# Reordering the first batch of an attention, Fourier mix and feed-forward kernel by changing the durations in its order model

## The chip, the cores and the metric

The kernel runs on one core of one Trainium2 chip. A core has five engines that work side by side, each through its own queue in program order: TensorE (PE, with its weight loads shown apart as PEld), VectorE (DVE), ScalarE (ACT), GpSimd (POOL) and SyncE (SP). POOL and SP also issue the DMAs. The metric is the device time of one execution in microseconds.

## The reference

Eight batches of 12 heads, 448 positions and 64 features per head. A squared-ReLU attention is followed by a Fourier mix over both axes, a normalization and a feed-forward layer, with the un-normalized sum added back:

```python
scores = q @ k.T / sqrt(64)
x = (maximum(scores, 0) ** 2 / 448) @ v        # heads side by side: (8, 448, 768)
u = x + real(fft(fft(x, axis=1), axis=2))
un = (u - mean(u)) / sqrt(var(u) + 1e-6)
out = u + maximum(un @ w_ch1, 0) @ w_ch2        # 768 -> 3072 -> 768
```

## The kernel before

Everything is on the chip at once as a pipeline over batches. For batch b, `load_group` fetches queries, keys and values of four heads at a time (three groups per batch) by DMAs that POOL issues. The heads are turned so that features lie on partitions: for batches 0 and 1 on TensorE (`turn_on_pe`, line 505, copied back at line 510), from batch 2 on by a VectorE reordering copy (line 469) and a transposing DMA on SP (line 481). `attention` makes, for each pair of heads m (six per batch) and each quarter c of the keys, a score (line 736, two matmuls on half the array each). ScalarE takes the ReLU (line 761), VectorE or ScalarE the square (lines 776, 773), and four quarters are multiplied with the values (line 718). `fold` scales the product and adds and subtracts its mirrored halves, which halves the work of the Fourier mix.

The mix multiplies with cosine and sine tables: `build_dft` makes them at the start, from indices that POOL writes (`dft_indices`, lines 245 to 251), with VectorE (lines 304 to 306) and ScalarE sines (line 310). For half of the channels the negated table is needed (line 333). Batch 0's channel products (`first_channels`, line 1187) run while its attention is going on. Then `first_tail` does the row products (lines 823, 827), the statistics (847), the scale, the normalization (900 to 905), the turn on TensorE (926) and the unload (941) for four tiles of rows. Its end makes the first feed-forward group ready. Feed-forward groups (`ffn`, lines 1452, 1477, 1503, 1583) are groups of 384, 512, 384 and then 256 rows. Their matmuls are what TensorE does most of the time, and attention of later batches is put between them.

The order of all instructions is not written by hand. Each piece is a Python generator that asks `need(engine, duration, dependencies, buffers)`. `Streams.run` picks, again and again, the request that could start first by its own clock of each engine, and the pieces issue their instructions in that order. So the durations (`mm`, `act`, `dve`, `SWITCH`, `LATENCY`), the times added to a load before it counts as ready (`ready`), and the ranks given to `sch.add` decide only the order in each engine's queue. On the chip every instruction still waits for its real data. A gate with the constant `LEAD` keeps later batches' attention from running too far ahead of the feed-forward work.

While TensorE has nothing to do in the order model before the first channel products are complete, `warming` issues short matmuls on zeros (line 1661), so that its clock stays up. There are three score banks (`BS`, one of them taken by the first channel products) and two feed-forward banks (`BF`), which the transposes, the value products and the fourth row tile also use. The software DMA queue of POOL works in order and has eight semaphores in turn, so a ninth DMA waits for the first.

The line that gives the time at which loads count as ready, and the keys' transposing DMA that waits in the model for the queries' landing:

```python
ready[i][x].t = sch.dma(e, GRP, 360e3, "sw") + (1.5 if g else 0.0, 3.0, 14.0, 7.0)[min(b, 3)]
...
for x in range(2):
    e = yield need("SP", 0.8, [e + LATENCY["DVE"]], [BQT] if x == 0 else [])
    nc.sync.dma_start_transpose(out=t, in_=qk[x])
    e = sch.dma(e + 0.5, R * 2048, 180e3)
```

Of the kernel before, what the change touches and what calls it, by code (L numbers as in the profile page):

```python
# [11 lines left out]
AF = mybir.ActivationFunctionType  # L12
# [46 lines left out]

LATENCY = {"PE": 0.28, "ACT": 0.18, "DVE": 0.16, "POOL": 0.2, "SP": 0.1}  # L60


class Streams:
# [29 lines left out]
    def run(self):  # L93
        end = {}
        while self.streams:
# [36 lines left out]
            self.engine[eng] = start + dur  # L132
# [28 lines left out]
SWITCH = 0.13  # L161
# [3 lines left out]
def kernel(  # L165
# [132 lines left out]
    def build_dft():  # L298
# [27 lines left out]
        for m in range(3):  # L326
# [5 lines left out]
            e = yield need("DVE", 0.3, [dft_ready])  # L332
            nc.vector.tensor_scalar(chan_neg[:, m], chan[m][:, :, KH:], -1.0, None, op0=ALU.mult)
            dft_ready.t = chan_ready[m].t = e + LATENCY["DVE"]

# [26 lines left out]
    def load_group(i, which=(0, 1, 2)):  # L362
# [3 lines left out]
        for x, (nm, src) in enumerate((("q", q), ("k", k), ("v", v))):  # L366
# [54 lines left out]
    def loading():  # L421
# [11 lines left out]
        yield from load_group(NG + 2, (2,))  # L433
        yield from load_w2([1, 2, 3])
# [22 lines left out]
    def turning():  # L457

        for b in range(B):
            for g in range(NG):  # L460
# [62 lines left out]
    def fold(b, m, F, av, give, av_end):  # L523
# [4 lines left out]
        def leave():  # L528
# [10 lines left out]
            if b == 0:  # L539
# [119 lines left out]
    def attention(b, left=None):  # L659
# [9 lines left out]
        while pa < NB:  # L669
# [38 lines left out]
            for part in ("scores", "values") if few else ("values", "scores"):  # L708
# [19 lines left out]
                for i in range(p, p + n):  # L728
                    m, c = divmod(i, 4)
                    qT, kT, flat = turned[b][m // 2]  # L730
                    wide = R if b < 2 else 128
                    k0 = (2 * c + m % 2) * R
                    sc = BS.take()
                    for h in range(2):
                        ps = slice(h * Dh, (h + 1) * Dh)
                        nc.tensor.matmul(sc[:wide, h, 0:S].rearrange("k (c q) -> k c q", c=4),  # L736
                                         lhsT=flat[ps, k0:k0 + wide], rhs=qT[ps, m % 2],
                                         start=True, stop=True)
# [4 lines left out]
                    if b == 0 and i == NB - 1:  # L743
                        first_scores.t = e
# [8 lines left out]

    def squares(b, scs, sqs):
        for i, sc, t in scs:
            e = yield need("ACT", act(2 * S) - 0.03, [t + LATENCY["PE"]], [BSQ])
# [42 lines left out]
    def first_tail(pcs):  # L799
# [88 lines left out]
        def norm(t, hf, en):  # L888
# [5 lines left out]
            d = {"ACT": act(D // 2), "DVE": dve(D // 2), "POOL": 2.0}[en]  # L894
# [12 lines left out]
            t_un[t][hf] = e + LATENCY[en]  # L907
            if min(t_un[t]) or en == "POOL":
                half_un[ch][i].t = max(t_un[t])
# [25 lines left out]
        def unload(t, en):  # L935
            n, idn, c0, w = turned_cols(t)
            g = groups[0][2]
            src = pts[t][0][:, :, 0:384].rearrange("p h (m w) -> p h m w", w=128)[:, :, :, 0:w]
            dst = g[:, :, c0:c0 + w].rearrange("p (h m) w -> p h m w", h=2)
            last = yield need(en, (act if en == "ACT" else dve)(6 * w), [done[t][0]])  # L940
            (nc.scalar.copy if en == "ACT" else nc.vector.tensor_copy)(dst, src)
            BS.give(pts[t][0], last)
# [774 lines left out]
```

## Time and profile before

| what | value |
|---|---|
| median of 3 runs | 584.73 us (584.64 to 585.35) |
| the profiled execution | 584.67 us, span 582.8 us |
| mean granted clock of TensorE | 0.997 |
| TensorE busy | 572.9 us (98% of the span) |
| VectorE, ScalarE, POOL busy | 406.4, 335.0, 133.7 us |
| moved by DMA | 81.85 MB, mean 140 GB/s |

The page has six parts: busy time of each engine, the span in 40 slices, the DMA queues, the chain of work that ended last, the costliest groups of instructions, and the DMA issues. Besides there are views that answer a question: busy time in chosen windows, a timeline of one engine, who waited for whom, and groups by line. In a timeline a row gives the start and length in microseconds, the engine, the line, the operation, output and inputs, and in brackets the idle time before it and what ended that. Rows of the same kind in a row are merged (x5). Matmuls overlap in the pipeline, so the length of one is more than its share of TensorE's time.

### The profile page before, as it was taken

The numbers are of one execution on the slowest core, as the hardware profiler recorded it, in microseconds if no ns is written. First come the engines' busy times: TensorE is split into PE (matmuls) and PEld (weight loads), VectorE is DVE, ScalarE is ACT, GpSimd is POOL, SyncE is SP. The second block draws the span as 40 slices with busy tenths as digits, with TensorE's granted clock in tenths as the row PEclk, the third lists the DMA queues.
The fourth block names the chain that finished last, engine by engine and source line by source line (L and its number), as shares of the span: only waits on it lengthen the run. The fifth ranks groups of instructions, "written<-read, shape, count | busy, mean of one in ns | idle before, by whom it ended". The sixth has DMA issues, their size and how long they took to land.

```text
span 582.8 us, 11457 instructions
## 1 busy us (share of the span) xinstructions
PE 572.9 (98%) x4476; PEld 365.7 (63%) x4476; DVE 406.4 (70%) x927; ACT 335.0 (57%) x511; POOL 133.7 (23%) x188
## 2 busy tenths in 40 slices
PE   8999999999999999999999999999999999999997
PEld 7566556544455546556857667568577786868684
DVE  5978667986669988787787878987946852222222
ACT  5866873587745787676668748777654340304040
POOL 8534021411115313421333032303300230000000
PEclk9998999999999999999999999999999999999999
DMA  9999999776947997699579987993433353031201
GB/s 120 206 211 227 222 210 134 173 131 95 181 57 189 207 172 168 116 216 167 122 123 207 180 153 147 200 176 115 126 75 100 118 151 99 30 94 36 79 30 55
DMA packets 133493, 81.85 MB, mean 140 GB/s; under 512 B 77504, under 2 KB 128704, under 8 KB 133440
## 3 DMA queue, kind: packets, MB, share of 16 engines
q0 software_dynamic: 40320, 33.63, 38.2%
q1 hardware_dynamic: 93120, 47.50, 36.3%
q8 instruction: 35, 0.57, 0.4%
q14 instruction: 18, 0.15, 0.1%
HBM read 62.91 MB, written 26.25 MB: 153 GB/s over the span
## 4 chain that ended last, share of the span: by engine, by line
PE 88%; DVE 6%; ACT 4%; issue 1%; POOL 0%; DVEq 0%; ACTq 0%; POOLq 0%
PE psF L1452 37%; PE psF L1583 26%; PE psS L736 6%; PE psF L718 5%; PE psF L1503 3%; PE psF L1477 3%; PE psS L1212 2%; ACT sq L761 2%; DVE sq L776 2%; PE psS L718 1%; PE psS L823 1%; PE psS L1026 1%; PE psS L1187 1%; PE psF L505 0%; ACT un L1087 0%
## 5 line engine op out<-in xcount | busy, mean ns | idle before, releaser
L1452 PE MATMUL psF<-unT,w 128*128 128x256 bf16 (+2 forms) x1728 | 229.8, 291 | 1.2 <-ACT unT L999 0.9
L1452 PEld LDWEIGHTS <-w 128*128 128x128 bf16 x1728 | 165.9, 98 | 61.6 <-issue 11.5
L761 ACT ACTIVATE sq<-psS 112x896 bf16<-112x896 f32 x192 | 164.4, 918 | 38.4 <-PE psS L736 38.0
L1426 ACT ACTIVATE hT<-psF 128x512 bf16<-128x512 f32 (+3 forms) x169 | 87.9, 532 | 116.6 <-PE psF L1452 115.8
L776 DVE TENSOR_TENSOR sq<-sq 112x896 bf16<-112x896 bf16 x161 | 100.6, 638 | 16.6 <-ACT sq L761 15.6
L1583 PEld LDWEIGHTS <-hT 128*128 128x128 bf16 x792 | 76.0, 98 | 54.4 <-issue 5.8
L1438 DVE TENSOR_TENSOR o<-psF,o 128x384 f32<-128x384 f32 x92 | 50.9, 553 | 44.8 <-PE psF L1583 39.6
L1583 PE MATMUL psF<-w,hT 128*128 128x384 bf16 x462 | 81.7, 326 | 0.3 <-DVE hT L1424 0.2
L736 PE MATMUL psS<-qkT 64*128 64x448 bf16 (+1 forms) x384 | 51.6, 359 | 1.2 <-ACT qkT L510 0.4
L718 PE MATMUL psF<-sq,vn 112*64 112x448 bf16 x320 | 37.9, 358 | 0.3 <-DVE o L1438 0.3
L557 DVE TENSOR_SCALAR xT<-psF 128x224 bf16<-128x224 f32 x58 | 19.8, 383 | 26.3 <-PE psF L718 26.2
L376 POOL DMA_DIRECT2D vn<-in_v_dram x24 | 17.3, 720 | 76.0 <-PE psS L736 67.7
L1059 POOL TENSOR_TENSOR u<-tp,xn 112x385 f32<-112x385 f32 (+2 forms) x14 | 13.3, 953 | 93.1 <-DVE tp L1041 81.5
L1583 PE MATMUL psF<-wsum,hT 128*128 128x384 bf16 x198 | 34.6, 326 | 0.0
L736 PEld LDWEIGHTS <-qkT 64*128 64x128 bf16 (+1 forms) x384 | 15.9, 102 | 28.7 <-issue 21.2
L376 POOL DMA_DIRECT2D qn<-in_q_dram x21 | 15.5, 739 | 69.9 <-DVE qkr L469 49.6
L718 PEld LDWEIGHTS <-vn 112*64 112x64 bf16 x384 | 17.8, 109 | 21.4 <-issue 13.7
L773 ACT ACTIVATE sq<-sq 112x896 bf16<-112x896 bf16 x31 | 29.5, 956 | 0.5
L1068 DVE BATCH_NORM_STATS2 stats<-u 112x6 f32<-112x384 f32 (+2 forms) x56 | 28.4, 541 | 0.0
L1087 ACT ACTIVATE un<-u,nmr,rstd 112x768 bf16<-112x768 f32 (+2 forms) x22 | 22.4, 1025 | 7.3 <-DVE nmr L1074 5.0
L1477 PE MATMUL psF<-w,hT 128*128 128x384 bf16 x144 | 25.1, 326 | 0.0
L1503 PE MATMUL psF<-w,hT 128*128 128x384 bf16 x144 | 24.7, 326 | 0.0
(166 smaller groups left out, 612.6 us busy)
## 6 DMA issues: line engine op xcount, KB each, us to landing
out_dram<-o SPq DMA_DIRECT2D x56, 192.0 KB, 2.2
vn<-in_v_dram POOLq DMA_DIRECT2D x24, 224.0 KB, 5.9
qn<-in_q_dram POOLq DMA_DIRECT2D x21, 224.0 KB, 5.3
kn<-in_k_dram POOLq DMA_DIRECT2D x21, 224.0 KB, 5.5
w<-in_moe_w_ch_dram POOLq DMA_DIRECT2D x12, 384.0 KB, 14.5
w<-in_moe_w_ch_dram POOLq DMA_DIRECT2D x4, 1152.0 KB, 20.5
utop<-u SPq DMA_DIRECT2D x12, 336.0 KB, 3.1
o<-utop SPq DMA_DIRECT2D x16, 192.0 KB, 3.8
```

What stands on the lines that cost most here:

```text
L376: nc.gpsimd.dma_start(out=t, in_=src[b, hs].rearrange("h (p j) d -> p h (j d)", j=4))
L718: nc.tensor.matmul(av[h * Dh:(h + 1) * Dh, 0:S], lhsT=vn[:, c, h0 + h, :], rhs=sq[:, h, :], start=(c == 0), stop=(c == 3))
L736: nc.tensor.matmul(sc[:wide, h, 0:S].rearrange("k (c q) -> k c q", c=4), lhsT=flat[ps, k0:k0 + wide], rhs=qT[ps, m % 2], start=True, stop= ...
L761: nc.scalar.activation(r, sc[:R, :, 0:S], AF.Relu)
L773: nc.scalar.activation(r, r, AF.Square)
L776: nc.vector.tensor_tensor(r, r, r, op=ALU.mult)
L1426: nc.scalar.activation(hs, ps, AF.Relu)
L1438: nc.vector.tensor_tensor(o, pc[:, 0:DH], o, op=ALU.add)
L1452: nc.tensor.matmul(ph[:, i * N:(i + 1) * N], lhsT=w1_sb[m][hf][:, (jj + i) * 128:(jj + i + 1) * 128], rhs=unT[:, m, 0:N], start=(m == 0), ...
L1477: nc.tensor.matmul(pc[:, 0:DH], lhsT=block(j, c), rhs=w2(j, hf), start=(j == 0), stop=(j == JC - 1))
L1503: nc.tensor.matmul(pc[:, 0:DH], lhsT=block(2 * i + k, c), rhs=weights[i], start=(start and i == 0), stop=(i == KP - 1), skip_group_check=True)
L1583: nc.tensor.matmul(pc[:, 0:DH], lhsT=lhs[i], rhs=rhs[i], start=(start and i == 0), stop=(i == KP - 1), skip_group_check=True)
```

## The change

Batch 0's attention becomes two streams: `first_attention` issues scores one at a time, `first_values` multiplies each quarter of the keys with the values as soon as that quarter is squared. Constants of the order model change: matmul, ScalarE and switching durations are shorter, `OVERLAP` lets an engine take the next instruction a little before the end of the last, the extra times of loads from batch 2 on go from 14 and 7 to 2 and 1, `LEAD` goes from 2.6 to 2.8. The negation of the tables moves from VectorE to POOL, the index writing goes ahead of the identity and of the first values' load, the last pair's scaling in batch 0 and the last unload are split over ScalarE and VectorE, the fourth tile's statistics go ahead of the third's scale, the fourth tile's copies behind its unload. Three of the four loads of the second weight matrix wait for the third tile's normalization. From batch 2 on the keys' transposing DMA counts as ready when the copies are done, not when the queries' transpose has landed. The second weight matrix counts as free for overwriting after the last whole chunk, not after each.

```diff
+OVERLAP = {"ACT": 0.12, "DVE": 0.07}
...
-            self.engine[eng] = start + dur
+            self.engine[eng] = start + max(dur - OVERLAP.get(eng, 0.0), 0.5 * dur)
...
-    return n / 2400 + 0.006
+    return n / 2400 + 0.002
...
-    return n / 1200 + 0.2
+    return n / 1200 + 0.17
...
-SWITCH = 0.13
+SWITCH = 0.1
...
-            e = yield need("DVE", 0.3, [dft_ready])
-            nc.vector.tensor_scalar(chan_neg[:, m], chan[m][:, :, KH:], -1.0, None, op0=ALU.mult)
-            dft_ready.t = chan_ready[m].t = e + LATENCY["DVE"]
+            sch.add(negative(m, dft_ready.t), (0, 0))
+
+    def negative(m, t):
+        e = yield need("POOL", 0.4, [t])
+        nc.gpsimd.tensor_scalar(chan_neg[:, m], chan[m][:, :, KH:], -1.0, None, op0=ALU.mult)
+        dft_ready.t = chan_ready[m].t = e + LATENCY["POOL"]
...
-            ready[i][x].t = sch.dma(e, GRP, 360e3, "sw") + (1.5 if g else 0.0, 3.0, 14.0, 7.0)[min(b, 3)]
+            ready[i][x].t = sch.dma(e, GRP, 360e3, "sw") + (1.5 if g else 0.0, 3.0, 2.0, 1.0)[min(b, 3)]
             if i == 0 and x == 1:
-                yield need("POOL", 0.7)
-                make_identity(nc, ident)
-            if i == 0 and x == 2:
                 e = yield need("POOL", 1.1)
                 dft_indices()
                 indices_ready.t = e + LATENCY["POOL"]
+                yield need("POOL", 0.7)
+                make_identity(nc, ident)
...
+        yield need("POOL", 0.0, [first_norms])
         yield from load_w2([1, 2, 3])
...
-                ts = []
+                ts, copied = [], e + LATENCY["DVE"]
                 for x in range(2):
-                    e = yield need("SP", 0.8, [e + LATENCY["DVE"]], [BQT] if x == 0 else [])
+                    e = yield need("SP", 0.8, [copied], [BQT] if x == 0 else [])
...
-            if b == 0:
+            if b == 0 and m == MC - 1:
+                t1 = yield need("ACT", act(HS), [av_end], [BX[m]])
+                nc.scalar.activation(xa[0], xa[1], AF.Copy, scale=1.0 / (64.0 * S))
+                t = yield need("DVE", dve(HS), [av_end])
+                nc.vector.tensor_scalar(xb[0], xb[1], 1.0 / (64.0 * S), None, op0=ALU.mult)
+                t = yield need("DVE", 2 * dve2(NS), [t1 + LATENCY["ACT"]])
+            elif b == 0:
...
+    def first_attention():
+        F, sqs = [], {}
+        for i in range(4 * MC):
+            m, c = divmod(i, 4)
+            e = yield need("PE", mm(S) + 2 * SWITCH, [turned_at[0][m // 2][m % 2]], [BS])
+            sc = score(0, i)
+            if i == 4 * MC - 1:
+                first_scores.t = e
+            sqs[i] = [None, Cell(), None]
+            sch.add(squares(0, [(i, sc, e - SWITCH)], sqs), (0.2, 0.2))
+            if c == 3:
+                if m % 2 == 1:
+                    BQT.free.append(e)
+                sch.add(first_values(m, F, sqs), (0.1, 0.1))
+
+    def first_values(m, F, sqs):
+        vn, h0 = loads[m // 2][2], 2 * m % HG
+        for c0, c1 in ((0,1),(1,2),(2,3),(3,4)):
+            e = yield need("PE", (c1 - c0) * mm(S) + 2 * SWITCH, [sqs[4 * m + c][1] for c in range(c0, c1)] + [ready[m // 2][2]],
+                           [BF] if c0 == 0 else [])
+            if c0 == 0:
+                av = BF.take()
+            for c in range(c0, c1):
...
+                for h in range(2):
+                    nc.tensor.matmul(av[h * Dh:(h + 1) * Dh, 0:S], lhsT=vn[:, c, h0 + h, :], rhs=sq[:, h, :],
+                                     start=(c == 0), stop=(c == 3))
...
         yield from stats(3, 0)
+        yield from stats(3, 1)
+        yield from aggregate(3)
         yield from scale(2)
         yield from norm(2, 0, "POOL")
-        yield from stats(3, 1)
-        yield from aggregate(3)
...
+        yield from turn(3, 0)
+        yield from unload(3, "ACT", 0)
+        yield from unload(3, "DVE", 1)
         yield from copy(3, 0, "ACT")
-        yield from turn(3, 0)
-        yield from unload(3, "DVE")
         yield from copy(3, 1, "DVE")
...
-            w2_free.t = e + LATENCY["PE"]
+            if c == WHOLES[b][-1]:
+                w2_free.t = e + LATENCY["PE"]
...
-    LEAD, MIXED, SPARE, ELASTIC = 2.6, 1, 0.5, (1, 99)
+    LEAD, MIXED, SPARE, ELASTIC = 2.8, 1, 0.5, (1, 99)
...
-        sch.add(attention(0), (0, 0))
+        sch.add(first_attention(), (0, 0))
```

More of the change, by code (lines that the diff above doesn't have):

```diff
@@ L729, in attention @@
                     m, c = divmod(i, 4)
[L730 to L738, printed above, removed]
+                    sc = score(b, i)
                     scs.append((i, sc, e - SWITCH - (4 * mm(S) + SWITCH if values and few else 0.0)
@@ L752, in attention, with score @@
                 yield from fold(bv, mv, Fv, av, give, av_end)
+    def first_attention():
[20 more added lines that the diff above has]
+            for c in range(c0, c1):
+                sq, _, at = sqs.pop(4 * m + c)
+                sq_ids.append((e, at))
+                BSQ.free.append(e)
+                for h in range(2):
+                    nc.tensor.matmul(av[h * Dh:(h + 1) * Dh, 0:S], lhsT=vn[:, c, h0 + h, :], rhs=sq[:, h, :],
+                                     start=(c == 0), stop=(c == 3))
+        if m % 2 == 1:
+            BQ[2].free.append(e)
+        yield from fold(0, m, F, av, lambda when: BF.give(av, when), e - SWITCH + LATENCY["PE"])
+    def score(b, i):
+        m, c = divmod(i, 4)
+        qT, kT, flat = turned[b][m // 2]
+        wide = R if b < 2 else 128
+        k0 = (2 * c + m % 2) * R
+        sc = BS.take()
+        for h in range(2):
+            ps = slice(h * Dh, (h + 1) * Dh)
+            nc.tensor.matmul(sc[:wide, h, 0:S].rearrange("k (c q) -> k c q", c=4), lhsT=flat[ps, k0:k0 + wide],
+                             rhs=qT[ps, m % 2], start=True, stop=True)
+        return sc
     def squares(b, scs, sqs):
         for i, sc, t in scs:
-            e = yield need("ACT", act(2 * S) - 0.03, [t + LATENCY["PE"]], [BSQ])
+            e = yield need("ACT", act(2 * S), [t + LATENCY["PE"]], [BSQ])
             at = min(sq_ids)
@@ L893, in norm @@
                 deps.append(u_done[ch][i])
-            d = {"ACT": act(D // 2), "DVE": dve(D // 2), "POOL": 2.0}[en]
+            d = {"ACT": act(D // 2), "DVE": dve(D // 2), "POOL": 1.0}[en]
             e = yield need(en, d, deps, [BUN[ch]] if i == 0 and hf == 0 else [])
```

20 lines of the change are left out of this document (13 added, 7 removed).

## The prediction

> **What bounds the kernel now.** I read the page's summary first, then the windows of two stretches, then the waits of TensorE, then the timeline of the first stretch engine by engine.
>
> ```profile
> span 582.8 us, 11457 instructions
> PE 572.9 (98%) x4476; PEld 365.7 (63%) x4476; DVE 406.4 (70%) x927; ACT 335.0 (57%) x511; POOL 133.7 (23%) x188
> ...
> 4.40:39.60 35.20, 34.03 (x437) 22.56 (x435) 31.39 (x74) 26.62 (x35) 18.90 (x52) 1.00 1.19 194
> 0.00:54.00 54.00, 49.81 (x596) 34.41 (x597) 42.25 (x106) 37.76 (x56) 32.20 (x73) 1.00 1.13 190
> 54.00:583.00 529.00, 523.12 (x3881) 331.25 (x3879) 364.14 (x822) 297.26 (x456) 101.51 (x115) 1.00 0.71 135
> ...
> PE psF L1452 <- ACT unT L999: 0.9, 1, 0.9
> PE psF L718 <- DVE o L1438: 0.3, 1, 0.3
> ```
>
> Columns of a windows row: the stretch, its length, then busy time of PE, weight loads, DVE, ACT and POOL, granted clock, DMA share, GB/s. From 54 us on TensorE is busy for 523.1 of 529.0 us, and its longest wait for another engine is 0.9 us. So this long part is bound by TensorE's own work, which the change leaves alone: counted in the instruction streams, only 102 of the 202 short filler matmuls of `warming` go. What can move is the first 54 us. There TensorE's 49.8 us are partly filler, and the stage is a chain through VectorE and ScalarE. Whatever the first feed-forward matmul gains there, the end gains, unless the long part gets new waits.
>
> ```profile
> 2.93 0.24 POOL masks.py:197 MEMSET ident<- 128x128 bf16 x1
> 3.50 0.71 POOL L376 DMA_DIRECT2D vn<-in_v_dram  x1
> 4.21 0.17 POOL L245 IOTA drow<- 128x2 f32 x1
> 4.41 0.38 DVE L314 TENSOR_SCALAR drow<-drow 128x2 f32<-128x2 f32 x1 [3.19 <-POOL drow L245]
> 13.81 0.27 DVE L333 TENSOR_SCALAR channeg<-chan 128x386 bf16<-128x386 bf16 x1 [0.38 <-ACT chan L310]
> 13.99 0.41 DVE L304 TENSOR_SCALAR dftr<-dcol,drow 128x386 int32<-128x386 f32 x1
> 17.70 0.68 DVE L542 TENSOR_SCALAR xT<-psF 128x224 bf16<-128x224 f32 x2
> 23.55 2.76 DVE L776 TENSOR_TENSOR sq<-sq 112x896 bf16<-112x896 bf16 x5
> 38.26 0.69 DVE L542 TENSOR_SCALAR xT<-psF 128x224 bf16<-128x224 f32 x2 [0.96 <-PE psF L718]
> 39.25 0.27 DVE L589 TENSOR_TENSOR fold<-xT 128x225 bf16<-128x225 bf16 x1
> ...
> 16.36 0.95 PE L718 MATMUL psF<-sq,vn 112*64 112x448 bf16 x8
> 53.63 1.88 PE L1452 MATMUL psF<-unT,w 128*128 128x384 bf16 x6
> 91.71 2.11 PE L1477 MATMUL psF<-w,hT 128*128 128x384 bf16 x12
> ```
>
> Between 4.4 and 39.6 us VectorE is busy for 31.4 of 35.2 us, more than ScalarE (26.6), so it is the first bound of the stage, and 3.8 us of it is waiting. After the last fold at 39.5 the mix and the normalization of batch 0 follow, and the first feed-forward matmul issues at 53.63.
>
> **The change part by part.**
>
> *Iotas ahead of the identity and of the values' load.* VectorE starts at 4.41 because POOL reaches the first iota at 4.21, behind the memset at 2.93. Moved to the front they start at 2.93: 4.21 - 2.93 = 1.28 us earlier. The queue position of the later loads stays, only batch 0's first value load goes about 0.9 us back. Its landing isn't on the path, since the first value product issues only at 16.4. Bounds: 0, if VectorE then waits for the second group's queries and keys, to -1.28. I take -1.28.
>
> *The three negations of the table on POOL.* VectorE's slot for one is 13.99 - 13.81 = 0.18 us; taking the other two the same, three free 0.5 us. Price on POOL: its queue now waits for ScalarE's sines between loads, so the first weights' load is issued perhaps 2 us later. That is covered by the backlog in the DMA queue, as this shows:
>
> ```profile
> 17.16 3.48 POOL L406 DMA_DIRECT2D w<-in_moe_w_ch_dram  x6
> 21.27 0.53 POOL L406 DMA_DIRECT2D w<-in_moe_w_ch_dram  x1 [0.63 <-DMA qn<-in_q_dram]
> w<-in_moe_w_ch_dram POOLq DMA_DIRECT2D x12, 384.0 KB, 14.5
> 44.95 0.15 DVE L867 RECIPROCAL rstd<-std 128x1 f32<-128x1 f32 x1
> 45.13 0.16 DVE L868 SCALAR_TENSOR_TENSOR nmr<-mv,rstd 128x1 f32<-128x1 f32 x1
> 46.25 0.98 POOL L900 TENSOR_SCALAR un<-u,rstd,nmr 128x768 bf16<-128x768 f32 x1
> 46.78 0.46 DVE L868 SCALAR_TENSOR_TENSOR nmr<-mv,rstd 128x1 f32<-128x1 f32 x1
> ```
>
> A weight load takes 14.5 us from issue to landing, nearly all of it queueing. Without that cover the loads behind would land 2 us later; their first use is near 50, so still nothing. A second price: the same small VectorE operation takes 0.16 us alone and 0.46 while POOL works. Three such clashes cost 0.9 us, none 0; I take 0.3, one clash. Net -0.2, between -0.5 and +0.4.
> By the Trainium skill, "SBUF — State Buffer", section "Who interferes with whom", whoever issues first holds the shared port pair for the whole instruction and the other blocks. By that rule each negation could hold up one VectorE square for its own length, an estimate of 0.5 us from half the 0.98 us row, and the item would read +1.0 instead of -0.2.
>
> *Two streams instead of score groups.* `first_attention` issues scores as their buffers come free, and `first_values` takes one key chunk at a time where `attention(0)` took four after one another. Same matmuls.
>
> ```profile
> ACT sq L761 <- PE psS L736: 2.0, 4, 0.7
> DVE sq L776 <- ACT sq L761: 1.0, 5, 0.2
> 37.27 0.95 PE L718 MATMUL psF<-sq,vn 112*64 112x448 bf16 x8
> 35.08 0.92 ACT L761 ACTIVATE sq<-psS 112x896 bf16<-112x896 f32 x1 [0.40 <-PE psS L736]
> ```
>
> ScalarE waited four times, 2.0 us, for scores that stood behind a four-chunk product or fillers. At the end of the stage the last product ran 0.95 us and VectorE sat idle 0.96 us for it; with three chunks done before, a quarter remains: -0.7 us. Against it, ScalarE and VectorE now do most of the table work first, so the first squares come late and VectorE waits for the first ones. Bounds: -2.9 (all other waits of the 3.8 go as well: 3.8 - 0.96) to +1.5 (two more table operations' worth of waiting early); I take -0.7, the wait that is seen.
>
> *Last fold leaves through two engines.* Two operations of 0.68 us together become one on each: -0.3 us, on the path.
>
> *The normalization's tail.*
>
> ```profile
> 48.52 0.16 DVE L867 RECIPROCAL rstd<-std 112x1 f32<-112x1 f32 x1
> 48.71 0.16 DVE L868 SCALAR_TENSOR_TENSOR nmr<-mv,rstd 112x1 f32<-112x1 f32 x1
> 48.79 0.56 DVE L847 BATCH_NORM_STATS2 stats<-psF 112x6 f32<-112x384 f32 x1
> 51.97 0.77 DVE L941 CAST unT<-psS 128x582 bf16<-128x582 f32 x1 [0.48 <-PE psS L926]
> ```
>
> The fourth tile's statistics go ahead of the third's scale (48.79 - 48.52 = 0.27 us) and its last unload (0.77 us) is halved over two engines (-0.3, with a fixed part left). Sum -0.6. The other way: the two copies of `u` now follow the unload, so the fourth tile's two banks come free for the feed-forward up to 0.5 us later. Range -0.6 to 0; I take -0.5.
>
> *Weights' second half behind the norms; keys' transpose issued earlier; loads believed ready 12 and 6 us earlier; LEAD 2.8.* All of it is order only. POOL issues batch 0's mirrored store ahead of three large weight loads. The bytes are the same, and they are needed by the second layer, at 91.7. In the order the scores of later batches stand earlier: batch 7's first at 215 us of feed-forward work instead of 230. For work that was not waiting this gains nothing; I put the one seen wait, 0.9 us, down as gone (the last transposes for the second group have 2.9 us of feed-forward work behind them instead of none), and bound new waits between 0 and 59 visits x 0.3 us = 18, the longest of the small waits above. Since that list has four other waits, all of 0.2 to 0.3 us, in some 60 visits, I take 59 x 0.03 = 1.8. Net +0.9.
>
> *Granted clock.*
>
> ```profile
> 13.00:16.40 3.40, 2.88 (x53) 1.90 (x52) 2.95 (x7) 2.91 (x5) 2.97 (x12) 1.00 1.45 194
> 50.50:53.90 3.40, 2.07 (x35) 1.44 (x35) 2.92 (x6) 3.27 (x6) 1.69 (x2) 1.00 1.13 252
> 53.90:57.30 3.40, 3.40 (x26) 1.63 (x24) 2.54 (x5) 1.22 (x2) 0.00 (x0) 0.50 1.26 209
> 57.30:60.70 3.40, 3.40 (x27) 1.71 (x24) 1.58 (x1) 3.17 (x5) 0.00 (x0) 1.00 1.16 207
> ```
>
> After a stretch with TensorE busy for 2.07 of 3.40 us the clock stood at 0.50 for the next 3.4 us, in which TensorE was always busy: 3.4 x 0.5 = 1.7 us lost. A stretch with 2.88 kept the clock. In the changed order five scores and four sets of eight transposes stand ahead of the first feed-forward matmul instead of two and two, and the tail is 0.5 us shorter, so this stretch should hold about 2.07 + 0.5 + 0.3 = 2.9 us. That is nearest the row that kept it: -1.7. Ends: -1.7 and, for a second such stretch, +1.7.
> The Trainium skill, "TensorE: Matmul & The Clock Gate", section "What's actually happening", names a free-running window of 3413 ns and half rate after an idle one. The length agrees with the row at 0.50; that the window must be idle doesn't, TensorE was busy in 60% of it.
>
> *Sum.* -1.3 - 0.2 - 0.7 - 0.3 - 0.5 + 0.9 - 1.7 = -3.8 us. The profiled execution took 584.67 us (span 582.8 and 1.9 around it), 0.06 below the median of 584.73, so the two are the same here: 584.7 - 3.8 = 580.9.
>
> **The rivals.**
> 1. *The stage loses its other waits too.* VectorE's 3.8 us of idle time go down to 0.9: 580.9 - 2.2 = 578.7, and 577 if the long part gets no new waits (-1.8). For it: the waits are short and many, which an order with truer durations can remove. Against: VectorE's first squares come later.
> 2. *Half the fillers are missed.* Place: the stage up to the first feed-forward matmul, where 102 filler matmuls no longer run. Three stretches at half clock in it, the one at 54 included, cost 3 x 1.7 = 5.1 against the forecast's none: 580.9 + 5.1 = 586.0, slower. It decides from the third stretch. For it: 2.88 busy us included fillers. Against: scores and values now alternate without gaps.
> 3. *The tight order meets late data.* Durations lost their margins, so each of some 59 visits of the attention to TensorE can now wait. At 0.1 us each (a third of the waits seen) it is 5.9 - 1.8 = +4.1: 585.0, no change; from 0.12 us each it is slower.
> 4. *The clock drop at the stage's end stays.* The 3.4 us stretch that decides may begin elsewhere relative to the work, and then hold the quiet part alone. For it: the fillers of the tail end at 50.0 as before. Against: the quiet part gets shorter. It gives -3.8 + 1.7 = -2.1, 582.6. The Trainium skill ("TensorE: Matmul & The Clock Gate", "What's actually happening") calls the window free-running.
>
> **How the numbers follow.** A change within 0.2%, 1.2 us, can hardly be told from none. Forecast (579.5 to 582) 0.42, rival 1 0.16, rival 4 0.16, rival 2 0.10, rival 3 0.16 (half of it slower than 585.9). Faster: 0.42 + 0.16 + 0.16 = 0.74, less 0.03 for rival 4 together with some late data: 0.71. Same: rival 3's lower half and that remainder, 0.08 + 0.03 = 0.11. Slower: rival 2 and rival 3's upper half, 0.18. The range leaves out rival 1's and rival 3's ends: 576.8 to 586.5.
>
> **What would show it.** VectorE's first operation near 3.2 us; the last fold near 36.5; the first feed-forward matmul near 50; no row with clock 0.50 between 9 and 60 us; TensorE's waits after 54 us under 4 us in all. Wrong if the clock falls inside the attention stage, if the first matmul is not before 52, or if waits for scores, loads or transposes appear behind 60 us.

## The result, and the profile after

| | before | changed |
|---|---|---|
| median of the runs, us | 584.73 | 592.99 (592.66 to 595.15) |
| profiled span, us | 582.8 | 591.2 |
| ratio, 95% interval | | 1.0153 [1.0132, 1.0173] |

The change makes the kernel 8.3 us slower; 3.8 us faster was forecast. The page's summary of the changed kernel:

```profile
span 591.2 us, 11260 instructions
PE 569.5 (96%) x4369; PEld 361.0 (61%) x4374; DVE 413.8 (70%) x923; ACT 331.7 (56%) x511; POOL 141.6 (24%) x193
```

TensorE has 3.4 us less to do (fewer fillers, no half clock) and the span is 8.4 us longer: the time went into waiting. VectorE is 7.4 us busier with four instructions fewer. The windows of the two stretches (columns as before), first of the changed kernel, then of the kernel before:

```profile
0.00:54.90 54.90, 48.18 (x517) 31.22 (x518) 44.79 (x105) 39.63 (x60) 36.45 (x76) 1.00 1.07 175
57.00:592.00 535.00, 519.45 (x3844) 328.93 (x3846) 366.94 (x816) 289.96 (x449) 105.14 (x117) 1.00 0.69 134
```

```profile
57.00:583.00 526.00, 520.12 (x3868) 329.92 (x3864) 362.00 (x818) 296.16 (x455) 101.51 (x115) 1.00 0.71 135
```

From 57 us to the last instruction the idle time of TensorE went from 5.7 to 14.8 us, +9.1 (the windows reach 0.2 and 0.8 us past it). The matmuls' ends overlap, so a finer measure is used from here on: the time from the start of one matmul to that of the next, less the n / 2400 us that the order model's `mm` gives its n columns, where more than 20 ns are left. These gaps sum to 21.2 us before and 31.9 after, +10.7. What TensorE waited for after 57 us in the changed kernel (total, times, longest):

```profile
PE psF L1510 <- DVE xT L568: 4.2, 4, 1.9
PE psF L1510 <- DVE stats L1126: 1.9, 1, 1.9
PE psF L1562 <- DVE o L1496: 1.3, 1, 1.3
PE psS L1270 <- DVE fold L647: 1.2, 1, 1.2
PE psF L1642 <- DVE o L1496: 0.9, 2, 0.6
PE psF L1510 <- DVE hT L1482: 0.6, 1, 0.6
PE psS L799 <- DMA qkT<-qkr: 0.3, 1, 0.3
```

Before, this list held 1.8 us; now, with two entries of 0.2 not shown, 10.8. All large entries name VectorE: a tile that should leave a feed-forward bank (xT, o, hT), or a statistic or a fold, comes late.

The start, in three timelines of the changed kernel (VectorE; GpSimd; the first feed-forward matmul on TensorE):

```profile
3.26 0.96 DVE L315 TENSOR_SCALAR drow<-drow 128x2 f32<-128x2 f32 x1 [2.04 <-POOL drow L246]
4.34 0.36 DVE L305 TENSOR_SCALAR dftr<-early,drow 128x240 int32<-128x240 f32 x1
37.24 0.27 DVE L600 TENSOR_TENSOR fold<-xT 128x225 bf16<-128x225 bf16 x1
43.39 0.16 DVE L917 SCALAR_TENSOR_TENSOR nmr<-mv,rstd 128x1 f32<-128x1 f32 x1
45.05 1.41 DVE L917 SCALAR_TENSOR_TENSOR nmr<-mv,rstd 128x1 f32<-128x1 f32 x1
```

```profile
20.61 1.55 POOL L338 TENSOR_SCALAR channeg<-chan 128x386 bf16<-128x386 bf16 x1
22.11 4.38 POOL L410 DMA_DIRECT2D w<-in_moe_w_ch_dram  x8
44.70 0.72 POOL L381 DMA_DIRECT2D vn<-in_v_dram  x1 [1.09 <-DMA w<-in_moe_w_ch_dram]
45.47 0.98 POOL L949 TENSOR_SCALAR un<-u,rstd,nmr 128x768 bf16<-128x768 f32 x1
```

```profile
51.47 0.40 PE L799 MATMUL psS<-qkT 64*112 64x448 bf16 x2
54.50 1.15 PE L1510 MATMUL psF<-unT,w 128*128 128x384 bf16 x6
```

The last fold ends at 37.5 instead of 39.5 us, and the first nmr stands at 43.39 instead of 45.13. There the gain is lost: GpSimd's scaling, which needs this nmr, starts at 45.47, 1.9 us after it is ready, because the weight loads were issued from 22.1 us instead of 17.2 and a value load in front of it waits for their queue. The first score after the turns is only 0.6 us earlier than in the kernel before (51.47 for 52.04):

```profile
52.04 0.40 PE L736 MATMUL psS<-qkT 64*112 64x448 bf16 x2
```

The first feed-forward matmul is at 54.50 instead of 53.63, behind three scores and two sets of transposes (some 1.5 us) that came later before. The windows around it:

```profile
47.14:50.55 3.41, 2.42 (x35) 1.69 (x33) 3.13 (x9) 2.45 (x6) 3.17 (x4) 1.00 1.28 249
50.55:53.97 3.42, 2.85 (x50) 1.95 (x50) 2.71 (x7) 3.42 (x7) 1.91 (x3) 1.00 1.35 240
53.97:57.38 3.41, 3.20 (x24) 1.58 (x21) 3.41 (x7) 3.41 (x5) 0.00 (x0) 1.00 1.18 212
```

The half-clock stretch is gone in this execution. But it belonged to the profiled execution of the kernel before and not to every one. A stretch of 3.4 us at half in 583 us lowers the mean clock to 0.997, which that execution has. Of the 75 executions of the same kernel that the experiments below were compared with, 59 have 0.999 or 1.000 (median 584.25 us) and 16 have 0.994 to 0.997 (median 585.90 us). Of the five of the changed kernel two have 0.999, one 0.997 and two 0.991.

The balance of the two profiled executions: +0.9 (first matmul) - 1.5 (work done ahead) - 1.7 (clock) + 10.7 (gaps) = +8.4 us, the difference of the spans.

Two places where the gaps arise. First, VectorE's timeline at 121 us, and TensorE's after it:

```profile
124.94 0.43 DVE L474 COPY qkr<-qn 112x1024 bf16<-112x1024 bf16 x1 [3.79 <-DMA qkT<-qkr]
125.29 0.39 DVE L568 TENSOR_SCALAR xT<-psF 128x224 bf16<-128x224 f32 x1
```

```profile
126.03 0.39 PE L1510 MATMUL psF<-unT,w 128*128 128x512 bf16 x1 [1.86 <-DVE xT L568]
```

VectorE stands 3.79 us before a query copy, whose buffer the transposing DMA of the group before has not read yet; the xT that would free TensorE's bank is queued behind the copy. Second, at 180 us, VectorE, GpSimd and TensorE:

```profile
180.14 1.26 DVE L1117 TENSOR_TENSOR u<-qs,xn 112x385 f32<-112x385 f32 x1
181.32 1.19 DVE L1119 TENSOR_TENSOR u<-tp,xn 112x383 f32<-112x383 f32 x1
182.44 1.01 DVE L1496 TENSOR_TENSOR o<-psF,o 128x384 f32<-128x384 f32 x2
```

```profile
179.93 1.06 POOL L1117 TENSOR_TENSOR u<-tp,xn 112x385 f32<-112x385 f32 x1
180.95 1.15 POOL L1119 TENSOR_TENSOR u<-qs,xn 112x383 f32<-112x383 f32 x1
```

```profile
183.04 1.14 PE L1562 MATMUL psF<-w,hT 128*128 128x384 bf16 x6 [1.32 <-DVE o L1496]
```

VectorE's sums take 1.26 and 1.19 us while GpSimd makes its own, and the `o` addition behind them comes late. So two suspects, "copies" and "clashes", beside a third reading: the order is just too tight on VectorE.

### The profile page after: what moved, and what is told of

Read it like the earlier page. It is cut to its first block, busy times and chain, and to the rows that moved or that the text cites. A ratio compares the mean times of both kernels' runs of the same rounds, so it can differ in the third digit from the quotient of the medians.

```text
span 591.2 us, 11260 instructions
## 1 busy us (share of the span) xinstructions
PE 569.5 (96%) x4369; PEld 361.0 (61%) x4374; DVE 413.8 (70%) x923; ACT 331.7 (56%) x511; POOL 141.6 (24%) x193
## 4 chain that ended last, share of the span: by engine, by line
PE 74%; DVE 12%; DMA 6%; ACT 4%; issue 2%; POOL 2%; SPq 0%; DVEq 0%; POOLq 0%; ACTq 0%
PE psF L1510 32%; PE psF L1642 25%; PE psS L799 5%; DMA qkT<-qkr 4%; PE psF L729 4%; DVE sq L825 2%; PE psS L1270 2%; PE psF L1535 2%; ACT sq L810 2%; DMA w<-in_moe_w_ch_dram 2%; PE psF L1562 1%; PE psS L729 1%; DVE stats L1126 1%; DVE xT L568 1%; DVE u L1119 1%
## 5 line engine op out<-in xcount | busy, mean ns | idle before, releaser
L1484 ACT ACTIVATE hT<-psF 128x512 bf16<-128x512 f32 (+3 forms) x178 | 90.6, 524 | 124.6 <-PE psF L1510 122.5
L825 DVE TENSOR_TENSOR sq<-sq 112x896 bf16<-112x896 bf16 x164 | 104.7, 657 | 13.4 <-ACT sq L810 12.9
L1642 PE MATMUL psF<-w,hT 128*128 128x384 bf16 x462 | 81.7, 326 | 0.0
L729 PE MATMUL psF<-sq,vn 112*64 112x448 bf16 x272 | 32.2, 358 | 0.1
L1624 DVE TENSOR_TENSOR s<-hT 128x768 bf16<-128x768 bf16 x11 | 6.1, 554 | 31.9 <-ACT hT L1484 31.8
L1145 ACT ACTIVATE un<-u,nmr,rstd 113x768 bf16<-113x768 f32 (+2 forms) x20 | 20.3, 1026 | 13.3 <-DVE nmr L1132 9.1
L729 PEld LDWEIGHTS <-vn 112*64 112x64 bf16 x336 | 15.7, 109 | 19.3 <-issue 12.4
L822 ACT ACTIVATE sq<-sq 112x896 bf16<-112x896 bf16 x28 | 26.5, 952 | 0.3
L1562 PE MATMUL psF<-w,hT 128*128 128x384 bf16 x144 | 24.8, 326 | 1.3 <-DVE o L1496 1.3
```

The source lines that it names most:

```text
L729: nc.tensor.matmul(av[h * Dh:(h + 1) * Dh, 0:S], lhsT=vn[:, c, h0 + h, :], rhs=sq[:, h, :], start=(c == 0), stop=(c == 3))
L822: nc.scalar.activation(r, r, AF.Square)
L825: nc.vector.tensor_tensor(r, r, r, op=ALU.mult)
L1484: nc.scalar.activation(hs, ps, AF.Relu)
L1562: nc.tensor.matmul(pc[:, 0:DH], lhsT=block(2 * i + k, c), rhs=weights[i], start=(start and i == 0), stop=(i == KP - 1), skip_group_check=True)
L1642: nc.tensor.matmul(pc[:, 0:DH], lhsT=lhs[i], rhs=rhs[i], start=(start and i == 0), stop=(i == KP - 1), skip_group_check=True)
```

## Experiments: which edit

Each run is told with its median and its ratio to the kernel before on the same chip; the median of the kernel before lies between 583.7 and 585.0 us on these chips, and most executions of a kernel lie within 1 or 2 us of its median, some further off.

**e1, the stage alone.** The order model's constants and the key wait go back:

```
-OVERLAP = {"ACT": 0.12, "DVE": 0.07}      +OVERLAP = {}
-n / 2400 + 0.002, n / 1200 + 0.17, SWITCH 0.1   +0.006, 0.2, 0.13
-act(2 * S) for the ReLU before a square   +act(2 * S) - 0.03
-... (1.5 if g else 0.0, 3.0, 2.0, 1.0)    +(1.5 if g else 0.0, 3.0, 14.0, 7.0)
-LEAD 2.8                                  +LEAD 2.6
-need("SP", 0.8, [copied], ...)            +[copied if x == 0 else e + LATENCY["DVE"]]
```

> The changed kernel with the old durations, load offsets, lead and key wait in the order model; only the first batch's parts are new. If the loss sits in the order of the long part (theory): 584.7 - 1.7 for the clock - 0.6 for the stage = 582.4, and TensorE's waits after 54 us back near 2 us. If the new start itself shifts the later work into bad places (rival): above 590.

586.71 us, 1.0041 [1.0016, 1.0065]: neither. The stage gives nothing even alone; TensorE waits 2.4 us at 104.6 us for a transposing DMA, more than the 1.7 us that was expected of the clock. Most of the loss is not the stage's.

**e2, e3, e4, one part of the model undone each** (e2: the offsets; e3: the first three lines of the list above; e4: its last line).

> The changed kernel with the loads of batches 2 and later believed ready 14 and 7 us late again. If the query and key copies stand too early on VectorE because the loads are believed early: most of the 7.0 us of copies waiting for transposing DMAs goes and the time falls to 586 to 588. If durations or the key wait are the cause: 592 to 594.

> The changed kernel with the old durations (matmul, ScalarE, switch, no overlap) in the order model. If VectorE's queue is packed too tightly by the new durations, so that leaving tiles stand behind late work: 585 to 587, and the waits on xT and o fall from 7 us to under 3. If the offsets or the key wait are the cause: 592 to 594.

> The changed kernel in which the order model lets the keys' transposing DMA wait for the queries' landing again. If the copy buffer is believed free before the DMA has read it: the copies' 7.0 us wait falls to 4 or less and the time to 586 to 589. If the durations or the offsets are the cause: 592 to 594.

607.49 us (1.039 [1.0351, 1.043]); 602.94 (1.0315 [1.0284, 1.0347]); 588.53 (1.0064 [1.0039, 1.009]). Undoing the offsets or the durations makes it far worse, so these two aren't a cost of their own that could be taken out; only the key wait gives time back, 4.5 us. In e3 one query copy waited 6.54 us for its load, believed there, and TensorE 6.23 us for the xT behind it. In e2 TensorE waited 6.5 and 7.2 us near 205 and 215 us, and the clock was then at half for 17 us.

**e7, the key wait alone in the kernel before** (`[copied]` for both, the rest as before).

> The kernel before with one edit: the order model lets the keys' transposing DMA go without the queries' landing. If this edit costs by itself what it cost in the changed kernel (593.0 - 588.5 = 4.5): 588 to 590. If it costs only together with the new durations and offsets: 584 to 586.

Three executions have a median of 591.28 us, 7.5 above the kernel before on that chip; a fourth took 599.09, and the ratio, 1.0167 [1.0095, 1.0239], is wide. The edit costs by itself what it cost in the changed kernel, or more. At 266 us a key copy waits 3.56 us for a transposing DMA, an `o` addition stands behind it, and TensorE waits 2.7 us.

**e16, the constants alone in the kernel before** (durations, overlap, offsets, lead; key wait kept).

> The kernel before with the new durations, overlap, load offsets and lead in the order model; stage and key wait as before. If these constants bring VectorE and GpSimd together: VectorE's time lost in operations that run long between 100 and 330 us rises from 5 us to 9 to 12, and the time is 587 to 590. If the constants alone are harmless: 584 to 586.

596.73 us, 1.0203 [1.0177, 1.0229]: harmful, by more than expected. TensorE's gaps after 57 us rise from 21.2 to 34.0 us, and VectorE's lost time (defined below) from about 5 to about 8. The parts don't add up: 11.9 us for the constants alone and 7.5 for the key wait alone, 8.3 for the whole change.

**e8, a lead of 2.75 instead of 2.8.**

> The changed kernel with a lead of 2.75 instead of 2.8, a change without a meaning of its own, to see how far the time moves by chance of the order. If the loss is a property of the change: 591 to 595. If single orders differ by as much as the whole loss: below 589 or above 597.

593.71 us, 1.0156 [1.0127, 1.0184], with seven of the same gaps. The loss does not hang on this one value.

## Experiments: the same order, one cause taken away

**e5 and e6, copies.** The control leaves out two weight blocks, and the test has two buffers:

```
+            if hf == 1 and m >= 4:
+                w1_sb[m][1] = w1_sb[m][0]          # both kernels: block neither loaded nor given a tile
+                ... continue
-    tag=f"qkr{x}", bufs=QR
+    tag=f"qkr{x}" if (b * NG + g) % 2 == 0 else f"qks{x}", bufs=1      # e6
```

> The changed kernel, its order the same instruction by instruction, but two of the twelve 128x1536 weight blocks of the first layer are neither loaded nor given a tile: the second halves of blocks 4 and 5 are read from their first halves (the output is then not the reference's), which frees 6 KB per partition. A control for the next run. Every theory: 592 to 593.5, the copies' wait for transposing DMAs near 7 us, TensorE's wait for a leaving tile at 126 us near 1.9 us.

> The control with the query and key copies going to two alternating buffers, the order model still counting one, so that the order is the same and only the wait for the transposing DMA's read goes. If the copies standing in front of leaving tiles on VectorE are what stalls TensorE: the 7.0 us of copy waits go, the stalls they cause (2.0 us at 126 us, 1.4 at 260, others in part) go, and the time is 2.5 to 5 us below the control. If the order itself, whatever the buffer, is too tight on VectorE (clashes with GpSimd, late sums): within 1 us of the control.

589.85 us (1.0106 [1.0074, 1.0139]) and 589.99 (1.0103 [1.0072, 1.0134]). The expectation failed: all copy waits are gone in e6, with them the gaps at 101 and 124 us (0.6 and 0.9), and the profiled span is 1.1 us shorter (586.5 for 587.6); the medians don't tell them apart. The other gaps stayed where they were, to 0.1 us. The control was the surprise: two loads less gave 2 to 3 us (6.1 above the kernel before on that chip, where the changed kernel is 8.3 above it). The first feed-forward matmul came at 53.26 instead of 54.50, because GpSimd's scaling started at 43.76, not 45.47; and the gap at 260 us was not there, the copies waiting 3.8 us in all instead of 7.0, and TensorE's gaps sum to 29.5 us instead of 31.9.

**e9 and e13, clashes.** GpSimd's sums and scalings are cut, in the changed kernel (e9) and in the one before (e13):

```
+            k = KN if i == 0 else 16
+            if i: nc.gpsimd.memset(u[:n, k:KN], 0.0)
-            eng.tensor_tensor(u[:n, 0:KN], ts[i][:n, 0:KN], x[:n, 0:KN], op=ALU.add)
+            eng.tensor_tensor(u[:n, 0:k], ts[i][:n, 0:k], x[:n, 0:k], op=ALU.add)
...          (the second sum and the scaling likewise)
```

> The changed kernel, its order the same, but GpSimd's two-operand sums and its scalings of batches 1 and later run over 16 columns instead of 385 or 768 and memory is set for the rest (the output is then not the reference's). If VectorE's operations that run long beside GpSimd (the 0.55 us sums taking 1.26, a 0.62 us square taking 1.73) are what makes leaving tiles late after 180 us: the gaps at 183, 231, 237 and 247 us (4.3 us) shrink and the time is 587 to 590. If VectorE's queue is simply too full there: 592 to 593.

> The kernel before, its order the same, with GpSimd's two-operand sums and scalings of batches 1 and later over 16 columns and memory set for the rest (the output is then not the reference's). If operations of VectorE running long beside GpSimd cost only where the order has put leaving tiles behind them: 583.5 to 584.7, since TensorE waits there for 1.8 us in all after 54 us. If they cost in both kernels: 579 to 581, as much below as in the changed kernel (6).

586.92 us (1.0051 [1.002, 1.0083]) and 583.68 (0.9982 [0.9968, 0.9997]): 6.1 us less in the changed kernel, 1.1 in the kernel before, whose gaps stay at 21.2 us, so that TensorE didn't wait for these clashes there. In e9 the gaps at 183, 231, 237, 247, 289, 350, 353 and 401 us are all gone. The same stretch as above in e9:

```profile
178.12 0.55 DVE L1120 TENSOR_TENSOR u<-qs,xn 112x385 f32<-112x385 f32 x1
178.58 0.57 DVE L1125 TENSOR_TENSOR u<-tp,xn 112x383 f32<-112x383 f32 x1
179.08 0.55 DVE L1503 TENSOR_TENSOR o<-psF,o 128x384 f32<-128x384 f32 x1
```

1.26 and 1.19 us have become 0.55 and 0.57. As groups of VectorE between 100 and 330 us (total and mean ns of one), before, changed, and e9:

```profile
L776 DVE TENSOR_TENSOR sq<-sq 112x896 bf16<-112x896 bf16 x83 | 50.7, 623 | 6.6 <-ACT sq L761 6.3
L626 DVE TENSOR_TENSOR fold<-folds 128x684 bf16<-128x684 bf16 x16 | 8.2, 520 | 0.1
```

```profile
L825 DVE TENSOR_TENSOR sq<-sq 112x896 bf16<-112x896 bf16 x85 | 53.9, 649 | 4.3 <-ACT sq L810 4.2
L637 DVE TENSOR_TENSOR fold<-folds 128x684 bf16<-128x684 bf16 x16 | 9.3, 598 | 0.2
```

```profile
L825 DVE TENSOR_TENSOR sq<-sq 112x896 bf16<-112x896 bf16 x86 | 52.1, 619 | 5.6 <-ACT sq L810 5.3
L637 DVE TENSOR_TENSOR fold<-folds 128x684 bf16<-128x684 bf16 x16 | 8.2, 526 | 0.2
```

Summed over all VectorE operations of that stretch, the time by which each exceeds the lower quartile of its own form is about 5 us before, 11 in the changed kernel, and 2 in e9; how the operations are grouped moves these by 1 or 2 us. By the Trainium skill, "SBUF — State Buffer", section "Who interferes with whom", a VectorE instruction with two SBUF inputs contends with a GpSimd instruction that reads SBUF and not with one that only writes. The runs agree for the sums: those that ran beside GpSimd's took up to 1.26 us, and with memory sets for most of that work 0.55. The squares of the changed kernel's trace show it too. Four of them run beside a GpSimd sum and take 1.60 to 2.85 us, this one the longest; of the 106 with nothing beside them none takes over 0.63.

```profile
397.27 2.85 DVE L825 TENSOR_TENSOR sq<-sq 112x896 bf16<-112x896 bf16 x1 [0.21 <-ACT sq L810]
```

But not every read of GpSimd's does this: the three squares beside a negation took 0.61 us, and of five beside a scaling only one was long, 1.28. The edit also shortened GpSimd's own sums and scalings after 57 us, to 31.8 us from 37.7; what that alone is worth isn't parted from the clashes.

One gap stayed in e9, TensorE and VectorE:

```profile
257.54 0.46 PE L1277 MATMUL psS<-chan,fold 128*114 128x193 bf16 x3 [3.13 <-DVE fold L647]
```

```profile
251.80 0.43 DVE L474 COPY qkr<-qn 112x1024 bf16<-112x1024 bf16 x1 [3.42 <-DMA qkT<-qkr]
```

The fold that TensorE waits for stands behind the copies on VectorE: it is a copy again. Hence the run with both taken away.

**e15, both** (the edits of e6 and e9).

> The changed kernel, its order the same, with both edits: GpSimd's sums and scalings short, and two alternating buffers for the query and key copies with two weight blocks not loaded (the output is then not the reference's). If the two causes together are the loss of the long part: the 3.3 us wait at 257 us that stayed with short sums goes too, no TensorE gap over 0.6 us is left, and the time is 580 to 582.5. If something else is left: 584 or more.

```profile
span 579.0 us, 11289 instructions
PE 567.9 (98%) x4369; PEld 361.7 (62%) x4374; DVE 399.7 (69%) x923; ACT 331.3 (57%) x511; POOL 133.7 (23%) x227
```

582.22 us, 0.9967 [0.9937, 0.9996]. No TensorE gap over 0.45 us is left and the gaps sum to 20.7 us, as in the kernel before (21.2). In the same order the two causes are the whole loss of the long part, together with the 2.4 us of gaps that went with the loads left out (e5). The third reading falls: with its operations at their own length and no copy waiting VectorE keeps up with this order. That its median lies 2.6 us under the kernel before's isn't a gain of the change: 1.1 would go in that kernel too (e13), and 1.2 come from the loads left out (e5).

**e18 and e17, a later landing in the model.** The changed kernel, and the kernel before with the fillers of e14, believe the transposing DMAs later:

```
                     e = sch.dma(e + 0.5, R * 2048, 180e3)
+                e += 4.0                        # e17: 1.5
                 BQR.free.append(e)
```

> The changed kernel as it is, without the key wait, but the order model believing that a pair of transposing DMAs lands 4 us later. If the key wait helped only as a margin for the landing: 587 to 590, the copies' wait for DMAs 4 us or less. If the two DMAs following one another is what matters: 592 to 594.

> The kernel before with the twelve fillers, and the order model believing that a pair of transposing DMAs lands 1.5 us later than it did. If the copies' waits for these DMAs (6.1 us in the run with fillers) are what loses the 1.7 us of the start: 582.5 to 583.5. If any other order is worse than the kernel before's: 586 to 592.

586.26 us (1.0029 [0.9995, 1.0063]), 6.7 less than the changed kernel. After 57 us VectorE's copies hardly wait:

```profile
DVE qkr L474 <- DMA kn<-in_k_dram: 0.6, 1, 0.6
DVE qkr L474 <- DMA qkT<-qkr: 0.4, 1, 0.4
```

So the key wait was worth something as a margin for the landing. TensorE's gaps sum to 23.4 us, though VectorE's lost time is still about 8; as in e13, clashes can be there without TensorE waiting for them. More margin isn't better everywhere: e17 took 601.52 us (1.0288 [1.0254, 1.0322]); its copies wait for no such DMA, but near 205 and 210 us TensorE waits 2.6 and 3.6 us for squares, and the clock is at half for 20 us. A single order can be that much worse; why this one is stays open.

## Experiments: the start

**e10, the negations as memory sets** (`nc.gpsimd.memset(chan_neg[:, m], 0.0)`, same order).

> The changed kernel, its order the same, but GpSimd's three negations are replaced by setting the memory, which waits for no sine (the output is then not the reference's). If GpSimd's queue, held up by the negations, is what ate the stage's gain (first weight load at 22.1 us instead of 17.2, its part of the normalization late by 0.8 to 1.9 us): weight loads from about 18.5 us, first feed-forward matmul at 53.3 or earlier, time 590 to 592. If the loads are hidden: first feed-forward matmul at 54.5 and 592.5 to 593.5.

```profile
47.65:51.07 3.42, 2.34 (x27) 1.32 (x25) 2.88 (x6) 2.76 (x6) 3.32 (x4) 1.00 1.23 245
51.07:54.48 3.41, 3.35 (x39) 2.05 (x40) 2.70 (x6) 2.34 (x4) 0.00 (x0) 0.50 1.15 229
```

592.35 us, 1.0134 [1.0092, 1.0177]. The first half came true: weight loads from 18.3 us, GpSimd's scaling at 43.52, the first score after the turns at 49.98 instead of 51.47. But the first feed-forward matmul is at 54.39: in the profiled execution (591.82 us, mean clock 0.997) a half-clock stretch came at 51.07 and took the 1.5 us. It need not come: of the other three executions one has a mean clock of 1.000 and took 589.76 us, two have 0.991 and took 592.89 and 593.38.

**e12 and e11, the negations back on VectorE**, with the stage alone (e12) and in the changed kernel with the key wait back (e11).

> The stage alone (old durations, offsets, lead and key wait) with the three negations back on VectorE. If GpSimd's queue is what the stage lost its gain to: 586.7 - 1.2 = 585.5, and below 584 if the wait for scores at 104.6 us (2.5 us) goes as well, because the copies and transposes come earlier. If the new start puts the later work in worse places: 586 to 590.

> The changed kernel with the key wait back in the order model and the three negations back on VectorE. If the two costs found so far add up: 588.5 - 1.2 = 587.3; with the clock drop at 54 us still gone. If the order is disturbed again by the shift: 588 to 592.

586.02 us (1.0024 [1.0008, 1.0041]) and 603.97 (1.0348 [1.031, 1.0387]). In e12 GpSimd's queue is free (loads from 18.9 us), and the first matmul still comes at 55.39, so this alone doesn't bring the start ahead. e11 missed widely: its start has three half-clock windows from 11.9 us, the first after this one, and TensorE's gaps are some 37 us.

```profile
8.50:11.90 3.40, 1.68 (x19) 1.09 (x18) 2.67 (x7) 3.40 (x6) 3.40 (x17) 0.99 1.26 153
11.90:15.30 3.40, 3.40 (x24) 1.42 (x22) 2.53 (x5) 3.32 (x6) 2.06 (x5) 0.50 1.39 182
```

**e14, the kernel before with twelve fillers.**

```
+            for i in range(12 if t == 2 else 0):
+                nc.tensor.matmul(bank[0][:, 384:512], lhsT=warm[:, 0:128], rhs=warm[:, 0:128], start=True, stop=True)
```

> The kernel before with twelve 128x128 filler matmuls (12 x 0.055 = 0.66 us) after the third set of turns, in the 0.98 us in which TensorE waits for the next, unknown to the order model, so that the order is the same. If the half-clock stretch at 53.9 us follows from TensorE's 2.07 busy us in the 3.4 before it: 2.7 busy us keep the clock, and the time is 583.0 (584.7 - 1.7). If the stretch has another cause, or the work there waits for something else: 584.5 to 585.

```profile
50.40:53.80 3.40, 2.80 (x45) 1.89 (x43) 2.92 (x7) 3.27 (x6) 1.47 (x2) 1.00 1.14 258
318.64 0.43 DVE L469 COPY qkr<-kn 112x1024 bf16<-112x1024 bf16 x1 [4.08 <-DMA qkT<-qkr]
```

584.09 us, 1.0002 [0.9978, 1.0027]: no difference from the kernel before. The windows row shows the clock kept with 2.80 busy us, but not that the fillers kept it. In e13, where TensorE's order up to there is that of the kernel before, without fillers, it was kept after this window as well:

```profile
49.84:53.25 3.41, 2.15 (x40) 1.51 (x38) 2.89 (x6) 3.28 (x6) 1.98 (x2) 1.00 1.12 261
```

And of the 26 executions of the kernel before on this chip 21 have a mean clock of 0.999 or 1.000, so there was little for fillers to win. Beside the profiled execution of the kernel before, VectorE's copies come 1.8 us ahead at 206 us and 1.5 at 314. The next one, the second row, waits 4.08 us for its transposing DMA, stands where it stood in the kernel before (318.5), and two TensorE gaps of 1.05 and 0.77 us follow it. So even a gain that is there at the start isn't safe to the end. No run with the full computation beat the kernel before.

## Why the prediction was wrong

The balance (+8.4) beside the sum (-3.8): the clock's -1.7 came as forecast; the stage's five terms, -3.0 together, came to -0.6 (+0.9 - 1.5); the order-only term, +0.9, came to +10.7. So of the 12.2 us between them 9.8 are the order-only term's and 2.4 the stage's.

- *Order-only parts, "I take 59 x 0.03 = 1.8. Net +0.9".* This is the step that failed: it was +10.7 us of gaps. Its bounds, 0 and 18, held it, but the range ended at 586.5 and didn't carry them. The value was taken from the small waits of the kernel before, which tell how quiet that order is and not how quiet another will be. For the keys' wait the runs show a margin that was given away (e4, e7, e18); for the other constants only that the order without them is worse (e16), and why that order is worse was not taken apart. Rival 3 named the direction, not the form: not 59 waits of 0.1 us but some ten of 0.4 to 2.0, from copies placed before the transposing DMA has read their buffer, and from VectorE and GpSimd made to work at the same time. Keys' wait: 4.5 us in one kernel (e4), 7.5 in the other (e7). Clashes: 6.1 against at most 1.1 (e9, e13).
- *"The bytes are the same"; moving work that isn't waiting gains nothing.* So it was for TensorE's work. What moved was the neighbourhood of VectorE's work, which the prediction priced only in the stage.
- *Negations on POOL, -0.2, covered by the queue's backlog.* Wrong. One takes 1.3 to 1.55 us on GpSimd, the loads went back 5 us and not 2, and the cover didn't count the scaling that stands behind these loads in GpSimd's own queue. It cost about 1.5 us at the first score (e10). The other price it named, a square held up by each negation, wasn't paid: the three squares beside them took 0.61 us, their own length.
- *Iotas, -1.28.* The first table operation (128x240) came 0.57 us earlier (4.34 for 4.91); the multiplications before it took up to 0.96 us instead of 0.38 beside GpSimd's iotas.
- *Two streams and the last fold, with the iotas and negations -2.5 to the last fold.* It came 2.0 us earlier; the 0.5 that is missing is about what the iotas didn't give. (The lower bound of the two streams, 3.8 - 0.96, is 2.8, not 2.9.)
- *Tail, -0.5.* Not seen: two nmr operations took 1.41 and 1.09 us beside GpSimd's scalings.
- *Clock, -1.7.* As forecast in the two profiled executions, and in part luck. The term took one execution of the kernel before for all of them; 59 of 75 others have a mean clock that leaves no room for such a stretch, so there was less to win than 1.7. The reason given, more busy time in the window, isn't shown: e13 kept the clock after 2.15 busy us. Rival 4 is as near as the prediction said, as e10's profiled execution shows. Rival 2 didn't occur in the profiled execution of the changed kernel, but did in e11; two of the changed kernel's five executions have a mean clock of 0.991, as three stretches would give, and where they lie isn't known.
- Of the signs it named, VectorE's first operation (3.26) and the clock row came as forecast, and the last fold nearly (it starts at 37.24 for 36.5); the first matmul (54.50, not near 50) and TensorE's waits (10.8 us, not under 4) did not.

## What to carry to other kernels

When an order is planned from a cost model, a late constant can be a margin: price its removal by what the trace shows of the real landing, not by the quiet of the order that the margin made. Take causes away without moving the order (another buffer, a shortened operation) before undoing edits, because every undone edit is also a new order, here anywhere from 586 to 607 us. Before moving work to GpSimd, list what stands behind it in GpSimd's queue and which two-input VectorE operations will run beside it.

## What the runs showed of the hardware

A VectorE operation on 128x1 took 1.41 us beside a GpSimd scaling of 0.98, 0.16 alone; a sum beside a GpSimd sum 1.26 for 0.55; a square beside two of them 2.85 for 0.62, beside a negation 0.61. The negation of 128x386 took 1.30 to 1.55 us on GpSimd; VectorE's slot for it was 0.18. For the clock, TensorE's busy time in a 3.41 us window doesn't decide alone: after 2.34 us the clock fell (e10), after 2.15 (e13) and 2.42 (changed kernel) it stayed, and after this one of e4 it stayed too:

```profile
48.46:51.87 3.41, 2.02 (x31) 1.46 (x29) 1.10 (x4) 1.61 (x5) 2.54 (x4) 1.00 1.32 250
```

The Trainium skill, "TensorE: Matmul & The Clock Gate", section "What's actually happening", lets the clock fall after an idle window; here it fell after windows that were half to two thirds busy. What in the window counts isn't settled by these runs; nor is it settled by the order alone, since executions of one kernel differ in it.
